# Attention with normalised queries and keys, then a two-layer MLP: a written-out schedule instead of a planner, with moved multiplies, sums and unused matmuls

## The chip, the cores and the metric

One core of a Trainium2 chip runs the whole program. The metric is the device time of one execution in microseconds (us), given as the median of several executions. The engines are named as the profile names them: PE is TensorE (matmuls; PEld is its weight load), DVE is VectorE, ACT is ScalarE, POOL is GpSimd, SP is the queue that issues most DMAs.

## The reference

```python
# q, k, v: (8, 12, 448, 64) float32; w_in: (768, 2048); w_out: (2048, 768)
def rmsnorm(x, g):
    rms = np.sqrt(np.mean(x * x, axis=-1, keepdims=True) + 1e-06)
    return x / rms * g
q_n, k_n = rmsnorm(q, g_q), rmsnorm(k, g_k)
scores = np.matmul(q_n, k_n.transpose(0, 1, 3, 2)) / np.sqrt(64)
scores = scores - np.max(scores, axis=-1, keepdims=True)
attn = np.exp(scores)
attn = attn / (np.sum(attn, axis=-1, keepdims=True) + 1e-09)
o = np.matmul(attn, v)                          # per batch and head
x = o.transpose(0, 2, 1, 3).reshape(3584, 768)  # heads side by side
h = x @ w_in
out = np.maximum(0.01 * h, h) @ w_out
```

## The kernel before

**Units.** A unit `u` is four heads of one batch; there are 24 (`NU`), three to a batch (`NQ`). The 448 keys of a head are cut into 7 tiles of 64. Per unit, q and k are loaded, squared (`prep_sq` on ACT or `prep_sqp` on POOL), summed (`prep_ssq`, DVE), turned into a factor (`prep_rinv`, ACT), multiplied (`prep_norm`, DVE), and transposed into `qkT` by PE (`prep_tr`) or by a DMA that SP issues (`prep_trd`). This is done one to three units ahead.

**Steps.** In the main loop a unit has four steps `d`, which hold the score tiles (0), (1, 2), (3, 4) and (5, 6). A step issues `qk` (PE, line 199: four matmuls of 64x64 for a tile, side by side in the array) and `ex` (ACT, line 218: exp of a tile of 128x896). The scores lie in one of two PSUM slots, so tile t can be written when the exp of tile t-2 has been read, and tile 1 of a unit needs the exp of tile 0. At step 0 stands the shift of the softmax: `shift_max` takes the maximum of tile 0 (DVE, line 236) and makes a diagonal of it (line 238), PE multiplies that (`shift_mm`, line 248, or 254 in the early units), DVE takes the second maximum (line 249 or 255), and line 257 gives the bias `eb` that every exp of the unit waits for. Between the two, PE runs the products with v of the unit before (`pv`, line 367) and the sums over exp (`zcol`, line 307). `pv_out` (ACT, line 322) copies the product out behind the second maximum, in front of the first exp. The reciprocal of the sums goes through ACT and a DMA (`zcol_inv`), and `xmul_pool`, `xmul_sb` or `xmul` writes the finished `xt` of the unit (line 347 on POOL or DVE, line 376).

**Items.** PE time between the steps is filled by the MLP of the batches before, cut into items in a queue: `moe1` (6 matmuls of 128x448, line 389, then a Prelu on ACT that writes `gt`), `moe2` (half of the sum for half an output tile, 8 matmuls of 128x384, line 430), and the items i0 to i6 of `seven` (8 matmuls of 128x384 each, line 471), which make two output tiles at once from seven products in place of eight. `seven` needs sums of blocks of `gt`, `s1` to `s4` (DVE, lines 452 to 461), and its results are merged by DVE adds (line 478). In the last two batches `moe1` is replaced in part by `late1` (line 591), a scheme of seven products too, with Prelu at line 601. What an item leaves for DVE, ACT and SP goes into a list `pend`, and `flush` runs it at the start of the next item or at the end of the step.

**Who decides the order.** The order is that of the program text on each engine. How many items a step takes is worked out by `fill`: each item has a cost (1.13 for `moe1`, 0.575 for `late1`, 1.31 for the others), each step a weight (`WD`), and the queue is spread over the steps left until the next batch is pushed. `fill` also holds the step's `jobs` (preparation of later units, multiplies): after each item one job is issued, and what is left follows at the end, behind `flush`. `warm` issues matmuls of which nothing is used. After unit 23 the rest of the queue and the last batch run as a tail; there `hold` makes the PSUM banks a hand-kept list that `drop` gives back to.

Of the kernel before, what the change touches and what calls it, by code (L numbers as in the profile page):

```python
# [18 lines left out]
def kernel(  # L19
# [13 lines left out]
    B, H, S, D = q.shape  # L33
# [4 lines left out]
    NU = B * NQ  # L38
# [373 lines left out]
    pend = []  # L412
    L, R, LR = slice(0, HC), slice(HC, DM), slice(0, DM)

    def flush():
        while pend:
            pend.pop(0)()

    def out_tile():
        return opool.tile([P, DM], FP32, tag="ost", name="ost")  # L420

    def moe2(pair, t, half, part):
        flush()
        if half == 0 and part == 0:
            ost[0] = out_tile()
        if part == 0:
            ost[1] = aux([P, 512], FP32, "op2")
        op2 = ost[1]
        for ft in range(8 * part, 8 * part + 8):
            nc.tensor.matmul(op2[:, 0:HC], gt[:, ft, ds(col(t), P)], wout16[:, ft, ds(HC * half, HC)],  # L430
                             start=(ft == 0), stop=(ft == FT - 1))
# [16 lines left out]
    def gblock(t, j):  # L448
        return gt[:, HF * j:HF * j + HF, ds(col(t), P)]
# [11 lines left out]
        nc.vector.tensor_tensor(sa[:, 3, x], gblock(tt[0], 1)[:, x], sa[:, 1, x], op=ALU.subtract)  # L461

    def later(fn, *args):
        pend.append(lambda: fn(*args))

    def seven(pair, tt, nxt=None, last=False):
        g = {}

        def mm(bank, a, b, first):
            for f in range(HF):  # L470
                nc.tensor.matmul(bank[:, 0:HC], a[:, f], b[:, f], start=(first and f == 0), stop=(f == HF - 1), skip_group_check=not first)  # L471

        def bank(name):
            g[name] = aux([P, 512], FP32, name)
            return g[name]

        def add(dst, src, name):
            nc.vector.tensor_tensor(dst, g[name][:, 0:HC], src, op=ALU.add)

        def put(i, c):  # L480
            store(pair, tt[i], g["o"][i], c, last)

        def i0():
            flush()
            g["o"] = (out_tile(), out_tile())
            mm(bank("ma"), gblock(tt[0], 0), wblock(0, 0), True)
            later(lambda: nc.vector.tensor_copy(g["o"][1][:, L], g["ma"][:, 0:HC]))

        def i1():
            flush()  # L490
            mm(bank("mb"), sa[:, 1], tw[:, 1], True)
            later(lambda: add(g["o"][1][:, L], g["o"][1][:, L], "mb"))
            later(lambda: drop(g["mb"]))

        def i2():
            flush()
            mm(g["ma"], gblock(tt[0], 1), wblock(1, 0), False)
            later(lambda: nc.scalar.copy(g["o"][0][:, L], g["ma"][:, 0:HC]))
            later(lambda: drop(g["ma"]))
            if last:  # L500
                later(put, 0, L)

        def i3():
            flush()
            mm(bank("mc"), sa[:, 0], tw[:, 0], True)
            later(lambda: add(g["o"][1][:, R], g["o"][1][:, L], "mc"))
            if nxt:
                later(s1, nxt)

        def i4():  # L510
            flush()
            mm(bank("md"), sa[:, 2], tw[:, 2], True)
            later(lambda: add(g["o"][1][:, R], g["o"][1][:, R], "md"))
            if last:
                later(put, 1, R)

        def i5():
            flush()
            mm(g["mc"], sa[:, 3], wblock(1, 1), False)
# [59 lines left out]
    def late1(b, tail, after):  # L579
# [45 lines left out]
        def item(n, s):  # L625
            flush()
            if not g:
                start()
            if n == 1:
                mm(get(1, s), 1, s, x_b(b, 0, 0), True)  # L630
                later(lambda: copy(tmp["u"][:, s % 2], g[1, s][:, 0:S]))
            elif n == 2:
                mm(get(2, s), 2, s, x_b(b, 1, 0), True)
                later(lambda: vadd(tmp["u"][:, s % 2], g[2, s], tmp["u"][:, s % 2]))
                later(lambda: drop(g[2, s]))
                later(lambda: out_(s, 0, 0, tmp["u"][:, s % 2]))
            elif n == 7:
                mm(get(7, s), 7, s, xs[3], True)
                later(lambda: nc.vector.tensor_copy(tmp["v"][:, s % 2], g[7, s][:, 0:S]))
            elif n == 6:  # L640
                mm(g[1, s], 6, s, xs[2], False)
                later(lambda: vadd(g[7, s][:, 0:S], g[1, s], tmp["v"][:, s % 2]))
            elif n == 5:
                mm(g[1, s], 5, s, xs[1], False)
                later(lambda: vadd(tmp["v"][:, s % 2], g[1, s], tmp["v"][:, s % 2]))
                later(lambda: out_(s, 1, 1, tmp["v"][:, s % 2]))
            elif n == 4:
                mm(g[7, s], 4, s, xs[4], False)
                later(lambda: out_(s, 1, 0, g[7, s][:, 0:S]))
                later(lambda: drop(g[7, s]))  # L650
            else:
                mm(g[1, s], 3, s, x_b(b, 1, 1), False)
                later(lambda: out_(s, 0, 1, g[1, s][:, 0:S]))
                later(lambda: drop(g[1, s]))
            for fn in after.get((n, s), ()):
                pend.append(fn)

        return item

# [14 lines left out]
    def push(b):  # L674
# [24 lines left out]
                    items.append((0.575, lambda w=w: item(*w)))  # L699
        if odd:  # L700
            tt, tn = (3, 4), (5, 6)
            items += [(1.31, fn) for fn in seven(pair, tt, tn)]
            for n, x, fs in ((len(items) - 7, 1, (s3, s4)),) if late else ((8, 0, (s1, s2)), (10, 0, (s3, s4)), (FT - 1, 1, (s1, s2)), (FT, 1, (s3, s4))):
                c, fn = items[n]
                items[n] = (c, also(fn, *[lambda f=f, x=x: later(f, tt, half[x]) for f in fs]))
            items += [(1.31, fn) for fn in seven(pair, tn, None, b == B - 1)]
        else:
            tiles = (2,) if fast else (0, 1, 2)
            std = [lambda t=t, h=h, p=p: moe2(pair, t, h, p) for t in tiles for h in range(2) for p in range(2)]
# [6 lines left out]
            items += [(1.31, fn) for fn in std]  # L716
        queue.extend(items)

    WD = (3.6, 2.9, 2.8, 2.8)
    STEPS = ((0,), (1, 2), (3, 4), (5, 6))  # L720
    debt = [0.0]

    def narrow(u):
        return 4 <= u < NU - 1
# [1 line left out]
    def fed(u, d):  # L726
        return u % NQ == 0 and d == 3

    def fill(u, d, jobs):
        total = sum(c for c, _ in queue)  # L730
        left = WD[d] + 3.0
        uu, dd = u, d
        while True:
            dd += 1
            if dd == 4:
                uu, dd = uu + 1, 0
            if uu == NU or (fed(uu, dd) and (u > 3 or uu > 3)):
                break
            left += WD[dd]
        debt[0] += total * WD[d] / left  # L740
        while queue and debt[0] >= queue[0][0] * 0.5:
            c, fn = queue.pop(0)
            fn()
            debt[0] -= c
            if jobs:
                jobs.pop(0)()
        flush()
        for job in jobs:
            job()

# [20 lines left out]
    with tc.manual_schedule():  # L771
# [150 lines left out]
        load_v(5)  # L922
        qk(2, (2,))
        ex(2)
        warm(6, st[2]["pb"])
        qk(2, (3,))
        ex(2)
        trn(3, 0, vcopy)
        trn(3, 1, vcopy)
        xmul(1)  # L930
        prep_ssq(4)
# [30 lines left out]
        for u in range(3, NU):  # L962
            for d in range(4):
                if d > 0 or u > 3:
                    qk(u, STEPS[d])
                    if d == 0:
                        shift_max(u)
                        if u == 6:
                            xmul_sb(u - 2)
                        if narrow(u - 1):  # L970
# [48 lines left out]
                if u + 2 < NU:  # L1019
# [72 lines left out]
```

## Time and profile before

| | |
|---|---|
| median of 4 runs | 417.25 us (416.98 to 417.43) |
| the profiled execution, its own time | 416.57 us |
| its span, from first to last instruction | 414.7 us |
| PE busy | 399.1 us, 96%, 3817 matmuls |
| DVE busy | 307.3 us, 74% |
| ACT busy | 300.7 us, 73% |
| POOL busy | 68.5 us, 17% |
| granted TensorE clock | 1.00 |

The profile is of one execution, and its times count from the start of the span. A row of the timeline gives start, duration, engine, line and operation, the tiles written and read, how many instructions were merged, and in brackets how long the engine had been idle and what released it. Matmuls are pipelined and the end of each is modelled, so the idle time in brackets is shorter than the hole in the stream: the hole is read from start to start.

### The profile page before, as it was taken

Reading aid. Unit: us, or ns where it says so; the run is one execution under the profiler, and the core shown is the slowest. Engines: PE = TensorE matmul, PEld = TensorE weight load, DVE = VectorE, ACT = ScalarE, POOL = GpSimd, SP = SyncE. Lnnn points to the kernel's source line nnn. Section 1 sums busy time; section 2 is a strip of 40 time slices with the busy share of each in tenths; the row PEclk is TensorE's granted clock in tenths of the full one; section 3 lists DMA queues with packets and bytes.
Section 4 is the critical chain, followed back from the end, with each engine's and each line's share of the span. In section 5 each row is a group of like instructions: output and inputs, shape, how many; then the busy total and the mean of one; then the engine's idle time right before and its main releaser. Section 6 shows DMA issues by size and latency. Waiting matters only on the chain.

```text
span 414.7 us, 9343 instructions
## 1 busy us (share of the span) xinstructions
PE 399.1 (96%) x3817; PEld 218.8 (53%) x3817; DVE 307.3 (74%) x492; ACT 300.7 (73%) x470; POOL 68.5 (17%) x70
## 2 busy tenths in 40 slices
PE   8688999999999999999999999999999999999995
PEld 7444444554445544555455544455445557558863
DVE  5888898998888757866668757767669788557762
ACT  5898887677987699767887689867986657653600
POOL 1868432200020200010020100020001202000000
PEclk9999999999999999999999999999999999999999
DMA  6999999989566995677664995678552470033023
GB/s 206 279 237 246 240 250 146 230 176 205 138 154 92 225 236 101 150 181 174 158 157 69 222 200 132 172 143 190 157 102 47 120 162 6 10 74 77 2 56 98
DMA packets 71950, 62.41 MB, mean 150 GB/s; under 512 B 36324, under 2 KB 67044, under 8 KB 71908
## 3 DMA queue, kind: packets, MB, share of 16 engines
q1 hardware_dynamic: 61312, 49.62, 47.6%
q0 software_dynamic: 10272, 11.80, 18.2%
q8 instruction: 30, 0.49, 0.5%
q10 hardware_dynamic: 324, 0.39, 0.3%
q14 instruction: 12, 0.10, 0.1%
HBM read 45.61 MB, written 11.01 MB: 137 GB/s over the span
## 4 chain that ended last, share of the span: by engine, by line
PE 82%; DVE 10%; ACT 5%; issue 1%; DMA 1%; SPq 0%; DVEq 0%
PE hps L389 27%; PE sT L199 8%; PE sT L367 5%; PE ma L471 5%; PE md L471 5%; PE mc L471 5%; PE op L430 5%; PE bank L591 4%; PE bank L471 4%; ACT et L218 3%; PE mb L471 3%; DVE n L171 3%; PE zc L307 2%; PE sT L471 2%; PE bank L430 1%
## 5 line engine op out<-in xcount | busy, mean ns | idle before, releaser
L218 ACT ACTIVATE et<-sT,eb 128x896 f16<-128x896 f32 x166 | 159.3, 1008 | 26.7 <-PE sT L199 17.4
L389 PE MATMUL hps<-xt,win 128*128 128x448 f16 x600 | 121.0, 353 | 0.3 <-DVE xt L376 0.2
L389 PEld LDWEIGHTS <-win 128*128 128x128 f16 x612 | 56.8, 98 | 58.4 <-issue 10.0
L383 ACT ACTIVATE gt<-hps 128x448 f16<-128x448 f32 x100 | 53.9, 554 | 7.4 <-PE hps L389 6.4
L199 PE MATMUL sT<-qkT 64*64 64x448 f16 x664 | 52.5, 363 | 4.1 <-ACT et L218 2.8
L159 DVE TENSOR_REDUCE ssq<-sq 128x14 f32<-128x896 f32 (+2 forms) x49 | 50.1, 1057 | 0.4 <-ACT sq L148 0.4
L471 PEld LDWEIGHTS <-sa 128*128 128x128 f16 x352 | 32.8, 98 | 26.3 <-issue 6.1
L128 POOL DMA_DIRECT2D vt<-in_v_dram x24 | 17.9, 746 | 172.0 <-PE sT L367 165.3
L471 PEld LDWEIGHTS <-gt 128*128 128x128 f16 x264 | 25.2, 98 | 19.0 <-issue 2.4
L199 PEld LDWEIGHTS <-qkT 64*64 64x64 f16 x672 | 15.3, 104 | 37.3 <-issue 32.6
L322 ACT COPY x<-sT 128x896 f32<-128x896 f32 x16 | 14.5, 906 | 25.7 <-DVE sT L249 25.7
L347 POOL TENSOR_TENSOR xt<-x,rz 128x896 f16<-128x896 f32 x9 | 18.9, 2099 | 79.9 <-DMA rz<-zs 71.5
L171 DVE TENSOR_TENSOR n<-rq,rinv 128x896 f16<-128x896 f32 (+2 forms) x25 | 26.7, 1073 | 5.0 <-ACT rinv L165 5.0
L292 DVE TENSOR_TENSOR ea<-ea,et 128x896 f16<-128x896 f16 x27 | 16.9, 625 | 16.5 <-ACT et L218 15.6
L367 PE MATMUL sT<-et,vt 64*64 64x448 f16 x532 | 28.5, 349 | 0.3
L430 PE MATMUL op<-wout,gt 128*128 128x384 f16 x160 | 28.4, 326 | 0.0
L236 DVE TENSOR_REDUCE sT<-sT 128x1 f32<-128x896 f32 x22 | 24.1, 1093 | 3.5 <-PE sT L199 3.5
L367 PEld LDWEIGHTS <-vt 64*64 64x64 f16 x672 | 20.5, 107 | 11.3 <-issue 1.4
L171 DVE TENSOR_TENSOR n<-rk,rinv 128x896 f16<-128x896 f32 (+2 forms) x26 | 26.1, 1010 | 0.0
L430 PEld LDWEIGHTS <-gt 128*128 128x128 f16 x192 | 17.6, 98 | 14.4 <-issue 3.1
L471 PE MATMUL ma<-wout,gt 128*128 128x384 f16 x128 | 23.5, 326 | 0.0
L292 DVE TENSOR_TENSOR ea<-et 128x896 f16<-128x896 f16 x14 | 9.4, 672 | 11.8 <-ACT et L218 11.7
(144 smaller groups left out, 548.5 us busy)
## 6 DMA issues: line engine op xcount, KB each, us to landing
rq<-in_q_dram SPq DMA_DIRECT2D x24, 448.0 KB, 4.3
rk<-in_k_dram SPq DMA_DIRECT2D x24, 448.0 KB, 5.7
out_dram<-ost SPq DMA_DIRECT2D x52, 192.0 KB, 3.1
rz<-zs SPq DMA_DIRECT2D x76, 112.0 KB, 2.3
vt<-in_v_dram POOLq DMA_DIRECT2D x24, 224.0 KB, 5.0
win<-in_moe_w_in_dram POOLq DMA_DIRECT2D x8, 384.0 KB, 15.9
wout<-in_moe_w_out_dram POOLq DMA_DIRECT2D x2, 1536.0 KB, 28.9
out_dram<-ost SPq DMA_DIRECT2D x4, 96.0 KB, 2.1
```

The source lines that it names most:

```text
L159: nc.vector.tensor_reduce(buf(u, "ssq")[:, ti, :, c[0]:c[1]], buf(u, f"sq{ti}")[:, :, c[0]:c[1]], axis=AXL.X, op=ALU.add)
L171: nc.vector.tensor_tensor(buf(u, "n16")[:, ti, c[0]:c[1]].rearrange("p s a d -> p a s d"), src[:, :, c[0]:c[1]], buf(u, "rinv")[:, ti, :, ...
L199: nc.tensor.matmul(banks[a][64 * r:64 * r + 64, 0:S].rearrange("p (t x) -> p t x", t=NS), kT(u, r, a, t), qT(u, r, a), start=True, stop=True)
L218: nc.scalar.activation(s["et"][:, t], sT[:, :, 0:S], AF.Exp, bias=s["eb"], scale=1.0)
L236: nc.vector.tensor_reduce(s["spare"][:, 511:512], sT[:, :, 0:S], axis=AXL.XY, op=ALU.max)
L292: nc.vector.tensor_tensor(s["ea"], s["et"][:, 0] if t == 1 else s["ea"], s["et"][:, t], op=ALU.add)
L347: eng.tensor_tensor(xts[b][:, g], s["x32"], s["rz"], op=ALU.mult)
L367: nc.tensor.matmul(s["pv"][r][64 * a:64 * a + 64, 0:S], vts[u % NV][64 * r:64 * r + 64, a, t], s["et"][64 * r:64 * r + 64, t, a], start=(t ...
L383: nc.scalar.activation(dst, src, AF.Prelu, bias=0.0, scale=1.0, alpha=0.01)
L389: nc.tensor.matmul(hps[:, 0:S], win16[:, kt // 2, kt % 2, ts(ft, P)], xt[:, kt // 2, kt % 2], start=(kt == 0), stop=(kt == KT - 1))
L430: nc.tensor.matmul(op2[:, 0:HC], gt[:, ft, ds(col(t), P)], wout16[:, ft, ds(HC * half, HC)], start=(ft == 0), stop=(ft == FT - 1))
L471: nc.tensor.matmul(bank[:, 0:HC], a[:, f], b[:, f], start=(first and f == 0), stop=(f == HF - 1), skip_group_check=not first)
```

## The change

The planner is replaced by a table `PLAN` of items per step. Against the counts that the planner gave, it differs in these places: in unit 3 one `moe1` item moves from step 1 to step 2 (2, 1 becomes 1, 2), in unit 4 one moves from step 0 and one from step 1, so that steps 0 to 2 hold 1, 2, 2 in place of 2, 2, 1; and one item each moves forward from step 0 of units 12, 16 and 18 to step 3 of units 11, 15 and 17 (1, 3 becomes 2, 2).

`flush(keep=True)` at the end of step 3 keeps `s1` to `s4` back, and a new `flush()` issues them behind `shift_max` of the next unit, so they stand between the first maximum and the second. This concerns `s3` and `s4` at units 8, 14 and 20 (half of the blocks) and at units 12 and 18 (all of them). When item i4 falls into step 2, no job is taken between it and the merges. The x multiply of unit 5 (`xmul_sb`) moves in front of two `prep_norm`. In the opening part, while unit 2's scores run, there are 6 more unused matmuls in one place and 8 in another. In the late batches `moe2` takes its 16 blocks in another order, and the first item of the last `seven` is mixed with the second. In the tail, half of the last `xmul` moves behind item i4.

```diff
-    def flush():
-        while pend:
-            pend.pop(0)()
+    def flush(keep=False):
+        kept = [p for p in pend if keep and p[0] in (s1, s2, s3, s4)]
+        now = [p for p in pend if p not in kept]
+        pend[:] = kept
+        for fn, args in now:
+            fn(*args)
...
-    def moe2(pair, t, half, part):
+    def moe2(pair, t, half, part, late=False):
...
-        for ft in range(8 * part, 8 * part + 8):
+        fts = (0, 1, 2, 3, 4, 5, 8, 9, 10, 12, 13, 11, 14, 15, 6, 7) if late else range(FT)
+        for i in range(8 * part, 8 * part + 8):
+            ft = fts[i]
             nc.tensor.matmul(op2[:, 0:HC], gt[:, ft, ds(col(t), P)], wout16[:, ft, ds(HC * half, HC)],
-                             start=(ft == 0), stop=(ft == FT - 1))
+                             start=(i == 0), stop=(i == FT - 1))
...
         def i0():
...
-            mm(bank("ma"), gblock(tt[0], 0), wblock(0, 0), True)
+            ma = bank("ma")
+            if mixed:
+                mm(ma, gblock(tt[0], 0), wblock(0, 0), True, range(6))
+                mm(bank("mb"), sa[:, 1], tw[:, 1], True, range(4))
+            mm(ma, gblock(tt[0], 0), wblock(0, 0), True, range(6 if mixed else 0, HF))
...
         def i1():
             flush()
-            mm(bank("mb"), sa[:, 1], tw[:, 1], True)
+            mm(g["mb"] if mixed else bank("mb"), sa[:, 1], tw[:, 1], True, range(4 if mixed else 0, HF))
...
+        i4.merges = True
...
-            items += [(1.31, fn) for fn in seven(pair, tt, tn)]
+            items += [(1.31, fn) for fn in seven(pair, tt, tn, mixed=late)]
...
-    WD = (3.6, 2.9, 2.8, 2.8)
+    PLAN = ("2122", "1222", "2112", "2122", "3232", "3322", "2322",
+            "2322", "3232", "2222", "3323", "3232", "2322", "2322",
+            "3232", "2222", "3323", "3232", "2322", "4356", "5232")
...
     def fill(u, d, jobs):
...
-        debt[0] += total * WD[d] / left
-        while queue and debt[0] >= queue[0][0] * 0.5:
-            c, fn = queue.pop(0)
+        for n in range(int(PLAN[u - 3][d])):
+            fn = queue.pop(0)[1]
             fn()
-            debt[0] -= c
-            if jobs:
+            if jobs and not (d == 2 and hasattr(fn, "merges")):
                 jobs.pop(0)()
-        flush()
+        flush(keep=d == 3 and u < NU - 1)
...
-        warm(6, st[2]["pb"])
+        warm(12, st[2]["pb"])
         qk(2, (3,))
         ex(2)
         trn(3, 0, vcopy)
+        warm(8, st[2]["pb"])
         trn(3, 1, vcopy)
...
                         shift_max(u)
+                        flush()
...
                         job(prep_rinv, u + 2)
+                        if u == 6:
+                            job(xmul_sb, u - 1)
                         for ti in range(2):
                             job(prep_norm, u + 2, ALL, (ti,))
...
-                if d == 2 and u == 6:
-                    job(xmul_sb, u - 1)
...
-        xmul(NU - 1)
-        for i, ns in enumerate(((3, 1), (2, 4))):
+        xmul(NU - 1, (0,))
+        for i, more in enumerate((((xmul, NU - 1, (1,)), (x_sum, B - 1, 3), (x_sum, B - 1, 1)), ((x_sum, B - 1, 2), (x_sum, B - 1, 4)))):
             c, fn = queue[i]
-            queue[i] = (c, also(fn, *[lambda n=n: later(x_sum, B - 1, n) for n in ns]))
+            queue[i] = (c, also(fn, *[lambda m=m: later(*m) for m in more]))
```

More of the change, by code (lines that the diff above doesn't have):

```diff
@@ L463, in later, with seven, mm @@
     def later(fn, *args):
-        pend.append(lambda: fn(*args))
-    def seven(pair, tt, nxt=None, last=False):
+        pend.append((fn, args))
+    def seven(pair, tt, nxt=None, last=False, mixed=False):
         g = {}
-        def mm(bank, a, b, first):
-            for f in range(HF):
+        def mm(bank, a, b, first, fs=range(HF)):
+            for f in fs:
                 nc.tensor.matmul(bank[:, 0:HC], a[:, f], b[:, f], start=(first and f == 0), stop=(f == HF - 1), skip_group_check=not first)
@@ L655, in item @@
             for fn in after.get((n, s), ()):
-                pend.append(fn)
+                later(fn)
         return item
@@ L708, in push @@
             tiles = (2,) if fast else (0, 1, 2)
-            std = [lambda t=t, h=h, p=p: moe2(pair, t, h, p) for t in tiles for h in range(2) for p in range(2)]
+            std = [lambda t=t, h=h, p=p: moe2(pair, t, h, p, late) for t in tiles for h in range(2) for p in range(2)]
             if fast:
@@ L717, in push @@
         queue.extend(items)
-    WD = (3.6, 2.9, 2.8, 2.8)
+    PLAN = ("2122", "1222", "2112", "2122", "3232", "3322", "2322",
+            "2322", "3232", "2222", "3323", "3232", "2322", "2322",
+            "3232", "2222", "3323", "3232", "2322", "4356", "5232")
     STEPS = ((0,), (1, 2), (3, 4), (5, 6))
-    debt = [0.0]
     def narrow(u):
@@ L729, in fill @@
     def fill(u, d, jobs):
[L730 to L739, printed above, removed]
-        debt[0] += total * WD[d] / left
-        while queue and debt[0] >= queue[0][0] * 0.5:
-            c, fn = queue.pop(0)
-            fn()
-            debt[0] -= c
-            if jobs:
+        for n in range(int(PLAN[u - 3][d])):
+            fn = queue.pop(0)[1]
+            fn()
+            if jobs and not (d == 2 and hasattr(fn, "merges")):
                 jobs.pop(0)()
-        flush()
+        flush(keep=d == 3 and u < NU - 1)
         for job in jobs:
```

## The prediction

> **What bounds the kernel now.** I read the page first, then the waits of PE, then the timeline around each place that the diff touches.
>
> ```profile
> span 414.7 us, 9343 instructions
> PE 399.1 (96%) x3817; PEld 218.8 (53%) x3817; DVE 307.3 (74%) x492; ACT 300.7 (73%) x470; POOL 68.5 (17%) x70
> ...
> PEclk9999999999999999999999999999999999999999
> ```
>
> PE is busy all the way at full clock, so a reordering can win no more than the holes in PE's stream. I measure a hole from start to start: a set of four 64x64 matmuls follows the last after 0.19 us, a 128x448 after 0.19, a 128x384 after 0.163. After the opening (to 45 us) and before the drain (from 410.5 us) few holes are left.
>
> ```profile
> PE sT L199 <- ACT et L218: 2.8, 7, 0.5
> ...
> PE bank L430 <- ACT gt L601: 0.5, 1, 0.5
> ...
> PE bank L471 <- ACT gt L601: 0.2, 1, 0.2
> PE hps L389 <- DVE xt L376: 0.2, 1, 0.2
> ```
>
> The waits of PE: mostly a score tile that waits for an exp. The timeline shows where, first units 3 and 4 (51.84 - 51.09 - 0.19 = 0.56 hole; 65.16 to 65.91 is the same in unit 4), with the DVE work behind it:
>
> ```profile
> 51.09 0.38 PE L199 MATMUL sT<-qkT 64*64 64x448 f16 x4
> ...
> 51.84 0.38 PE L199 MATMUL sT<-qkT 64*64 64x448 f16 x4 [0.37 <-ACT et L218]
> ```
> ```profile
> 54.34 1.08 DVE L171 TENSOR_TENSOR n<-rk,rinv 128x896 f16<-128x896 f32 x1
> ...
> 55.34 1.09 DVE L236 TENSOR_REDUCE sT<-sT 128x1 f32<-128x896 f32 x1
> ...
> 56.47 0.29 DVE L238 TENSOR_TENSOR dg<-ident,sT 128x128 f16<-128x128 f16 x1
> ...
> 56.81 0.23 PE L254 MATMUL pb<-dg,onesp 128*128 128x128 f16 x1
> ```
>
> Unit 12, where one item moves out of step 0 and the sums go between the two maxima:
>
> ```profile
> 171.95 0.38 PE L199 MATMUL sT<-qkT 64*64 64x448 f16 x4
> ...
> 172.44 1.52 PE L367 MATMUL sT<-et,vt 64*64 64x448 f16 x28
> ...
> 174.27 0.71 POOL L128 DMA_DIRECT2D vt<-in_v_dram  x1 [14.25 <-PE sT L367]
> 174.60 0.22 PE L248 MATMUL sT<-dg,onesp 128*128 128x64 f16 x2
> ...
> 174.86 0.30 DVE L249 TENSOR_REDUCE sT<-sT 128x1 f32<-128x128 f32 x1 [0.31 <-PE sT L248]
> 175.19 0.91 ACT L322 COPY x<-sT 128x896 f32<-128x896 f32 x1 [1.13 <-DVE sT L249]
> ...
> 175.27 0.68 DVE L458 TENSOR_TENSOR sa<-gt 128x1024 f16<-128x1024 f16 x1
> ...
> 175.99 1.01 ACT L218 ACTIVATE et<-sT,eb 128x896 f16<-128x896 f32 x1
> ```
>
> The holes there: 0.28 in front of 172.44 (pv's slot waits for an exp) and 0.21 in front of 174.60 (line 248 waits for the diagonal, whose maximum stood behind `s2`). And ACT's copy, then the first exp, hang on the second maximum.
>
> **The change part by part.** PE does the same matmuls, plus 14 unused ones. The holes at the touched places: 0.56 in unit 3; 0.56 in unit 4; 0.29 at 93.9 (the first `moe1` of batch 1 waits for xt of unit 5: six matmuls take 93.16 to 94.67 where 1.22 would do); 0.49 in unit 12; 0.28 in unit 16 (236.15 to 236.64); 0.49 in unit 18 (as unit 12); 0.63 at 358.12 (six matmuls from 356.51 would end at 357.49); 0.37 at 393.09 (391.74 + 0.98 = 392.72); 0.23 at 374.34 (372.81 + 1.30 = 374.11). Sum 3.91 us, the most there is. Now each:
>
> *Unit 3.* With one item less in step 1, tile 4 is asked for 1.13 earlier, at 48.40; the exp of tile 2 ends at 48.13, so no hole. With two items in step 2, tile 6 comes at 51.26 and the exp of tile 4 ends near 50.65. The hole is gone, but DVE is the next: it is busy without a gap from 46.8 to 55.4 (sums of squares, `add_e`, two norms), so the first maximum of unit 4 stays at 55.34, the diagonal at 56.47, and line 254 at 56.81, where PE now waits 0.6. Gain 0 (at most 0.56).
>
> *Unit 4.* Unit 3's end stays, so step 0 starts as before; step 0 has one item less and the hole at 65.91 is covered by the second item of step 2 (tile 6 at 65.32, exp of tile 4 ends near 64.8). DVE follows this time: its norms end near 67.9, PE's tile for the maximum of unit 5 comes at 68.0 in place of 68.6. Gain 0.56.
>
> *x multiply of unit 5.* DVE is free for it at 91.06; the last of its four rz DMAs is issued near 88.2 and lands 2.3 us later, at 90.5. It ends at 92.1, 1.8 us before the fifth matmul. The norms behind it and the transposing DMA on SP go 1.0 us later, and behind that SP only has stores; the maximum of unit 7 (PE-bound, now at 94.9) finds DVE free at 94.6. Gain 0.29.
>
> *Units 12 and 18.* Let Q be the start of step 0's tile. Two items before Q let the exp finish: 0.28 won. `s2` is out before Q, so the maximum is PE-bound; as in unit 8 (110.43 to 112.07) the diagonal starts at Q + 1.64 and PE, which gets to line 248 at Q + 2.14 (112.57 there), doesn't wait: 0.21 won. But `s3` and `s4` now follow the diagonal: from Q + 1.84 (0.20 behind it, as 82.84 to 83.04), 0.60 each by the rows 175.27 and 175.87, so the second maximum starts at Q + 3.05, not Q + 2.41. The first exp gives its slot back 2.1 us after that (1.13 to 1.19 to its start, 0.90 on), at Q + 5.15. PE with two items comes at Q + 4.90 (unit 9, also two of 1.30, took 126.73 to 131.73, with 0.10 more of `zcol`). New wait 0.25: net 0.24 each, 0.48 together. ACT's work on the reciprocal and the rz DMAs go about 1.5 us later; the stores that now stand ahead of them on SP are issued by then, and the POOL multiply has until 191.7. Beside it a norm takes 1.68 in place of 1.08, for which unit 13 has 0.4 of slack: 0 to 0.2.
>
> *Units 8, 14, 20.* Half sums of 0.34 each: the second maximum at Q + 2.52, the slot back at Q + 4.62, PE with three items at Q + 5.71 (110.43 to 116.14). Nothing.
>
> *Unit 16.* Becomes what unit 10 is (two items, no sums), which has no hole: gain 0.28.
>
> *Late `moe2`.* Its first eight blocks are all written by 356; those of line 601 come last, at 359.4, and are ready at 358.06. Behind it, tile 1 of unit 23 needs an exp that ended at 356.05. Gain 0.63.
>
> *Mixed i0.* Four matmuls of i1 fill the 0.37. But i1's other four need `s2`, which still ends at 393.94 (Prelu 393.03, `s1`, `s2` of 0.42 each). They started at 394.07 before, and now at 394.0. Gain 0.07.
>
> *Tail multiply.* With half of `xmul` behind it, the merge that i6 waits for ends 0.5 earlier, so i6 starts at 374.11. The sums of x end as before to 0.1. Gain 0.23.
>
> *Costed at nothing.* The 14 unused matmuls, 0.057 each: 0.34 into the 0.55 hole at 33.49 (wait for zslot), 0.46 into the 0.60 at 34.82 (wait for a norm); without that cover 0.8. They bring nothing, the granted clock there is 1.00 already. i4's merge ahead of the norms (units 9, 12, 15, 18, 21): norm k and its transposing DMA end some 0.45 later, and the readers are the `qkT` scaling and sums of squares of step 1, whose results wait a step; up to 0.4 if that cover fails.
>
> Sum: 0.56 + 0.29 + 0.48 + 0.28 + 0.63 + 0.07 + 0.23 = 2.54. The profiled execution's own time is 416.57 (span 414.7 and 1.87 around it), so it would be 414.03; the median, 417.25, stands 0.68 above it and becomes 414.7.
>
> **A rule against this change.** DVE sums whose operands lie in SBUF can be held by POOL. In the trace the same line 458 of 128x512 takes 0.42 alone but 1.85 beside POOL's multiply (120.97, POOL at 120.37). The sums' new place, Q + 1.84 to Q + 3.05, is where POOL issues the load of v (Q + 2.04, 0.71 long). The Trainium skill, "SBUF — State Buffer", section "SBUF: two separate sides", says that DVE and GpSimd share a port pair as an exclusive lock held for a whole instruction, and that descriptor writing for a POOL-issued DMA needs it. By the rule `s4` could be held for the issue: some 0.8 more at units 12 and 18, a wait of 1.05 there, and a total of 2.54 - 1.6 = 0.9. The nearest row speaks for no hold: the multiply of two SBUF operands at 83.04 took 1.08 beside such an issue at 82.75, as alone; but it is float32, not a fast f16 sum. I take no hold, and keep 0.9 for the range.
>
> **The rivals.**
> - *More comes.* If DVE's chain in unit 3 shortens, or the second maximum isn't late: 2.54 + 0.56 = 3.1, at most 3.9: 414.2 to 413.35. Against it: the gapless DVE row up to 55.34. 12%.
> - *The lock holds, or a norm or merge comes late.* 0.9 to 1.7 gained: 416.35 to 415.55. 21%.
> - *It does not do what it says.* ACT or a DMA, not PE, sets the pace, and every hole closed opens at the next exp as in unit 3: within 0.8 of 417.25. Against it: holes of ACT (0.59 before several Prelus) follow PE. 6%.
> - *Slower: the held sums.* One mechanism: each pair of moved sums is held h, and the second maximum, ACT's copy and the first exp with it. Units 12 and 18 then wait 0.25 + h each (0.49 before), units 8, 14 and 20 wait h - 1.06. Against the other gains of 2.06 that is even at h = 1.14 and 0.83 slower from h = 1.31. With the hold of the row at 120.97 (1.43) it is 418.7. A v issue lasts 0.71 to 0.76, so h should stay below that. 3%.
>
> **How the numbers follow.** The forecast, with its own range of 414.2 to 415.4, has 58%. A measurement here can tell about 0.2%, 0.83 us, from no change: under 416.42 is faster. Faster: 58 + 12 + 19 of the second rival = 0.89; same 0.08; slower 0.03. The range leaves out part of the first rival and the last two: 413.4 to 416.4.
>
> **What would show it.** Right: no hole at the steps 3 of units 3 and 4, but PE waiting about 0.6 for the diagonal (line 254) in unit 4; in units 12 and 18 a new wait of about 0.3 of tile 1 for the first exp; no wait at the late `moe2`; about 0.3 for `s2` in i1. Wrong: `s3` or `s4` far longer than 0.68 or 0.42, the second maximum over 1 us after line 248, or new PE waits in units 8, 14, 20 or 13.

## The result, and the profile after

The changed kernel takes 416.55 us (median of 44 runs, 415.34 to 418.12), the kernel before 417.20 on the same chips (63 runs). The ratio is 0.9983, with a 95% interval of 0.9978 to 0.9989: 0.7 us gained (0.5 to 0.9), where 2.54 were forecast. It lies just outside the forecast range (413.4 to 416.4).

From the page of the changed kernel, the lines that answer to those of before:

```profile
span 415.2 us, 9374 instructions
PE 399.9 (96%) x3831; PEld 220.0 (53%) x3831; DVE 309.0 (74%) x492; ACT 300.0 (72%) x470; POOL 69.1 (17%) x70
...
PEclk9899999999999999999999999999999999999999
```

The span is longer than before (414.7), which the medians contradict. The reason is in slice 2 of the clock row, and the table of windows shows it (window, its length, PE, PEld, DVE, ACT and POOL busy with the number of instructions in brackets, then the granted clock, the DMA share and GB/s):

```profile
12.00:16.00 4.00, 2.67 (x34) 1.71 (x34) 3.66 (x7) 3.69 (x8) 3.27 (x4) 1.00 1.07 343
16.00:20.00 4.00, 3.16 (x34) 1.99 (x34) 2.89 (x6) 3.28 (x4) 4.00 (x6) 0.77 1.18 224
20.00:24.00 4.00, 4.00 (x63) 2.49 (x65) 3.37 (x8) 3.37 (x6) 2.58 (x5) 0.80 1.07 242
24.00:30.00 6.00, 4.67 (x72) 2.78 (x61) 5.44 (x8) 5.93 (x9) 3.31 (x3) 1.00 1.12 230
```

This execution had a reduced clock between 16 and 24 us, and the third matmul of line 254 came 1.25 us later than in the profile of before (0.60 of it was there by the first one, at 12 us). In the thirteen profiles besides that of before, the same matmul stands 0.07 to 2.09 us behind that of before; 0.07 to 0.87 where the clock stays at 1.00, 0.57 to 2.09 where it dips. So the opening differs between executions, and the work after it must be compared by itself. I do that from the matmul of line 254 in unit 4 to the last instruction: 357.9 us before, 357.1 after, a gain of 0.78 that agrees with the medians.

Where PE waits now (its waits: total, times, longest):

```profile
PE sT L199 <- ACT et L218: 2.1, 5, 0.5
PE sT L248 <- DVE dg L238: 2.0, 2, 1.4
PE pb L254 <- DVE dg L238: 1.6, 3, 0.6
...
PE sT L476 <- DVE sa L460: 0.2, 1, 0.2
```

Two of these were forecast: unit 4's wait for the diagonal (0.6, the longest of the three in the third line) and i1's wait for `s2` (the fourth line). The second line was not: 2.0 us in two places in front of line 248, in units 13 and 19. Start to start these holes are 0.68 and 1.43 us. The prediction had named a new wait in unit 13 as a sign of its being wrong. This is the end of unit 18 and the start of unit 19 on DVE, POOL and PE, in the timeline of the changed kernel:

```profile
280.36 0.56 DVE L483 TENSOR_TENSOR ost<-md,ost 128x384 f32<-128x384 f32 x1 [0.74 <-PE md L476]
280.83 1.08 DVE L171 TENSOR_TENSOR n<-rq,rinv 128x896 f16<-128x896 f32 x1
280.94 2.93 POOL L347 TENSOR_TENSOR xt<-x,rz 128x896 f16<-128x896 f32 x1 [9.41 <-DMA rz<-zs]
281.83 2.98 DVE L171 TENSOR_TENSOR n<-rk,rinv 128x896 f16<-128x896 f32 x1
...
285.86 1.09 DVE L236 TENSOR_REDUCE sT<-sT 128x1 f32<-128x896 f32 x1
...
286.98 0.29 DVE L238 TENSOR_TENSOR dg<-ident,sT 128x128 f16<-128x128 f16 x1
287.32 0.22 PE L248 MATMUL sT<-dg,onesp 128*128 128x64 f16 x2 [1.37 <-DVE dg L238]
```

And the same place in the kernel before:

```profile
277.17 2.08 POOL L347 TENSOR_TENSOR xt<-x,rz 128x896 f16<-128x896 f32 x1 [7.09 <-DMA rz<-zs]
279.84 1.09 DVE L171 TENSOR_TENSOR n<-rq,rinv 128x896 f16<-128x896 f32 x1 [0.31 <-ACT rinv L165]
281.32 1.08 DVE L171 TENSOR_TENSOR n<-rk,rinv 128x896 f16<-128x896 f32 x1
283.95 1.09 DVE L236 TENSOR_REDUCE sT<-sT 128x1 f32<-128x896 f32 x1
```

Before, POOL's x multiply was over (279.25) when the first norm began. Now it starts at 280.94, because `rz` landed later. The second norm takes 2.98 us instead of 1.08, and two merges, the maximum, the diagonal and line 248 follow it. Unit 13 is the same on a smaller scale: POOL at 184.96, the first norm 2.23 long.

By place, the prediction's sum and the profile:

| place | forecast gain | measured |
|---|---|---|
| unit 3, unit 4 | 0, 0.56 | 0, 0.56 |
| x multiply of unit 5 | 0.29 | 0.28 |
| units 12 and 18, each | 0.24 | 0.35 |
| unit 16 | 0.28 | 0.28 |
| late `moe2` | 0.63 | 0.63 |
| mixed i0 | 0.07 | 0.05 |
| tail multiply | 0.23 | 0.10 |
| unit 21 (hole of 0.19 before line 248 gone) | none | 0.19 |
| unit 13 | 0 to -0.2 | -0.68 |
| unit 19 | not named | -1.43 |
| sum | 2.54 | 2.80 - 2.11 = 0.69 |

### The profile page after: what moved, and what is told of

Its sections match the earlier page's. It is cut to its first block, busy times and chain, and to the rows that moved or that the text cites. A ratio compares the mean times of both kernels' runs of the same rounds, so it can differ in the third digit from the quotient of the medians.

```text
span 415.2 us, 9374 instructions
## 1 busy us (share of the span) xinstructions
PE 399.9 (96%) x3831; PEld 220.0 (53%) x3831; DVE 309.0 (74%) x492; ACT 300.0 (72%) x470; POOL 69.1 (17%) x70
## 4 chain that ended last, share of the span: by engine, by line
PE 84%; DVE 9%; ACT 4%; issue 2%; DMA 1%; SPq 0%; DVEq 0%
PE hps L389 27%; PE sT L199 9%; PE op L435 6%; PE sT L367 5%; PE ma L476 5%; PE bank L602 5%; PE bank L476 5%; PE mc L476 5%; PE md L476 4%; DVE n L171 4%; PE mb L476 3%; PE zc L307 2%; ACT et L218 2%; PE sT L476 1%; PE bank L435 1%
## 5 line engine op out<-in xcount | busy, mean ns | idle before, releaser
L171 DVE TENSOR_TENSOR n<-rk,rinv 128x896 f16<-128x896 f32 (+2 forms) x26 | 28.0, 1084 | 0.0
L148 ACT ACTIVATE sq<-rq 128x896 f32<-128x896 f32 (+2 forms) x18 | 16.3, 913 | 1.3 <-DMA rq<-in_q_dram 1.3
```

What stands on the lines that cost most here:

```text
L171: nc.vector.tensor_tensor(buf(u, "n16")[:, ti, c[0]:c[1]].rearrange("p s a d -> p a s d"), src[:, :, c[0]:c[1]], buf(u, "rinv")[:, ti, :, ...
```

## The experiments

The theory to test, S: the held sums `s3`, `s4` make the second maximum of units 12 and 18 late, with it ACT's copy and the reciprocal, so `rz` is issued later (in these units also behind two output stores on SP that stood behind it before). POOL's multiply then falls beside the norms and blocks them. Rivals: M, the merge moved ahead of the norms is enough to delay the maximum; O, the opening takes the gain back through the additional unused matmuls. D, F and C came later and are explained in their place. The flight of `rz` is the time from the start of its first DMA packet to the end of its last. In the expectations, times of an instruction fetch and of a flight count from an origin 0.25 us later than the timeline's.

**rz ahead of the stores.** `zcol_inv` is issued at once in two units, so `rz` stands ahead of the two stores on SP.

```diff
-                        if u < NU - 1:
+                        if u in (12, 18):
+                            zcol_inv(u - 1)
+                        elif u < NU - 1:
                             job(zcol_inv, u - 1)
```

> The changed kernel, with one thing moved: in units 12 and 18 the reciprocal and its four rz DMAs are issued ahead of step 0's first item, so that on SP they stand ahead of the two stores again, as before the change. Theory S (the stores ahead of rz on SP, with the later second maximum, make POOL's multiply late, and it then lies beside the two norms of DVE, which hold the maximum of units 13 and 19): POOL's multiply starts 1.9 us after the last rz issue, near 184 in unit 12 and 279.2 in unit 18 (184.96 and 280.94 now); the norms beside it take at most 0.6 more than 1.08 (now 1.15 and 1.90 more), PE's waits in front of line 248 in units 13 and 19 fall from 0.68 and 1.43 to 0.1 to 0.4 each: 1.3 to 1.9 us less than the changed kernel, 414.7 to 415.3. Theory M (the merge moved ahead of the norms alone makes the maximum late): no change, 416.5, both waits as now. Theory O (the opening takes back the gain, by the 14 more unused matmuls): no change of the total either, 416.5.

Measured: 415.33 us, ratio 0.9959 (0.9947 to 0.9970). A part of it came: unit 13 doesn't wait any more, unit 19 waits 1.32. Timeline of this kernel, unit 12 and then unit 18:

```profile
183.15 2.08 POOL L347 TENSOR_TENSOR xt<-x,rz 128x896 f16<-128x896 f32 x1 [7.57 <-DMA rz<-zs]
184.88 1.31 DVE L171 TENSOR_TENSOR n<-rq,rinv 128x896 f16<-128x896 f32 x1
...
279.11 2.08 POOL L347 TENSOR_TENSOR xt<-x,rz 128x896 f16<-128x896 f32 x1 [9.14 <-DMA rz<-zs]
279.28 2.87 DVE L171 TENSOR_TENSOR n<-rq,rinv 128x896 f16<-128x896 f32 x1
```

Read the ends: POOL ends at 185.23 and the norm at 186.19; POOL at 281.19, the norm at 282.15. Each norm ends 0.96 us after POOL, whenever it began. My expected excess of "at most 0.6" was wrong: a norm that meets the multiply waits for whatever is left of it.

What the order saved is not what I thought. The rows of SP alone in unit 12, in the changed kernel and here:

```profile
178.00 1.17 SPq L409 DMA_DIRECT2D out_dram<-ost  x2
179.59 3.46 SPq L337 DMA_DIRECT2D rz<-zs  x4
```
```profile
178.71 2.57 SPq L337 DMA_DIRECT2D rz<-zs  x4
181.33 1.25 SPq L409 DMA_DIRECT2D out_dram<-ost  x2
```

Both issues of `rz` begin 3.74 us after line 248, when ACT has the reciprocal. But in the changed kernel the first packet of `rz` moves 2.17 us after that, behind packets of the stores (179.18 to 182.06) and an instruction fetch among them (179.17 to 180.73); here after 1.20. In unit 18 these are 1.24 and 1.21, so there was nothing to save there. The multiply comes 0.94 us earlier against line 248 in unit 12, and 0.26 in unit 18. There the issue of `rz` was over at 275.61, but the multiply began 3.5 us later, not 1.9; so something else delays the landing.

**Sums behind the second maximum.**

```diff
                         shift_max(u)
-                        flush()
...
                             shift_mm(u)
+                            flush()
```

> The changed kernel with the held sums s3 and s4 not behind the first, but behind the second maximum and its bias. Theory S: the second maximum of units 12 and 18 comes 1.2 us earlier, 0.31 after line 248; tile 1's waits for the first exp (0.14 each) go; the stores still stand ahead of rz on SP, so that rz starts only 0.4 earlier and POOL's multiply by as much: 0.3 to 0.9 us less than the changed kernel, 415.7 to 416.3, with 0.4 to 1.2 left of the wait in unit 19. A rival, that the late second maximum alone is the cause: both waits go, 414.2. Theory M: only the 0.28 of the two tile waits, 416.3.

Measured: 415.89 us, ratio 0.9981 (0.9970 to 0.9992), not to be told from the changed kernel. Both waits of tile 1 are gone and the second maximum follows line 248 directly again, but the stores hold `rz` up instead; units 13 and 19 wait 0.86 and 1.09. So the late maximum alone is not the cause, and unit 13's wait did not shrink as S had it.

**The merge behind the first norm again.**

```diff
-            if jobs and not (d == 2 and hasattr(fn, "merges")):
+            if jobs:
```

> The changed kernel with i4's merge behind the first norm again, as before the change (units 9, 12, 15, 18, 21). Theory S: the first norm of units 12 and 18 starts 0.4 to 0.9 us earlier and the maximum behind it 0.35 to 0.47, since the idle time of DVE in front of that norm is used: 0.5 to 0.9 us less than the changed kernel, 415.6 to 416.0; the norms still take 1 to 1.9 us more beside POOL. Theory M: both waits in front of line 248 go, 2.1 us less, 414.4. If the move of the merge was of use somewhere (units 9, 15, 21): 0.2 to 0.4 more in these, seen as new waits there.

Measured: 415.63 us, ratio 0.9968 (0.9957 to 0.9979). Waits of 0.54 and 0.54: smaller, not gone, so M alone is out, and the moved merge has a share in the waits. (The median itself can't be told from that of the changed kernel's second run, below.) Unit 12 here shows the other direction of the conflict:

```profile
183.68 1.09 DVE L171 TENSOR_TENSOR n<-rq,rinv 128x896 f16<-128x896 f32 x1 [0.32 <-ACT rinv L165]
183.86 2.86 POOL L347 TENSOR_TENSOR xt<-x,rz 128x896 f16<-128x896 f32 x1 [8.59 <-ACT rinv L165]
...
185.16 2.52 DVE L171 TENSOR_TENSOR n<-rk,rinv 128x896 f16<-128x896 f32 x1
```

The norm began first and took its 1.09; POOL's multiply was the one that was stretched, to 2.86 from 2.08, and the next norm then waited for it.

**Without the additional unused matmuls.**

```diff
-        warm(12, st[2]["pb"])
+        warm(6, st[2]["pb"])
...
-        warm(8, st[2]["pb"])
```

> The changed kernel without its 14 additional unused matmuls. Theory S: the opening of the changed kernel's profile (1.25 us later than before by 20 us, all of it ahead of these matmuls) is chance of that execution, and the 14 matmuls lie in waits: the time stays at 416.5 within 0.2, waits of 0.55 and 0.60 near 34 to 36 us instead of 0.22 each. Theory O: 1.2 us less, 415.3. If they keep the clock up behind them: more, and a granted clock under 1.00 after 35 us.

Measured: 414.94 us, ratio 0.9956 (0.9941 to 0.9971). S said no change here, and missed by 1.6 us. But O isn't right either: at the place of these matmuls nothing was won (unit 4's line 254 stands 0.09 behind that of before in this profile, 0.12 in the run with the merge moved back, which has the matmuls). What differs is unit 19, which doesn't wait: POOL's multiply started there at 278.19, counted from unit 18's line 248 that is 1.6 us earlier than in the changed kernel. The DMA queues show why. This is the changed kernel while `rz` of unit 18 is in flight, 275.9 to 280.1 (queue, packets, MB, share of 16 engines):

```profile
q1 hardware_dynamic: 816, 0.86, 80.6%
q8 instruction: 1, 0.02, 2.0%
q14 instruction: 1, 0.01, 0.5%
```

A packet of 16 KB of instructions falls into it. There are 30 of these in a run, 0.9 to 1.8 us long, and from one to the next PE runs 253 of its 7662 matmuls and weight loads on average, so I take them for PE's instruction fetches (7662 / 30 = 255 instructions each). `rz` goes in 512 packets of 896 bytes, and POOL waits for the last. With a fetch inside, the flight of `rz` in unit 18 took 3.3 to 4.4 us (eight profiles); without, 2.65 to 2.77 (six). Theory F: 28 PE instructions more, matmuls and weight loads, move the fetches earlier against the work, and in unit 18 into that flight. Theory D: the matmuls cost time directly. C: they keep the clock up.

**The unused matmuls alone, on the kernel before** (the two `warm` lines of the change).

> The kernel before with the 14 additional unused matmuls of the change and nothing else. Theory D (direct price): the run without them was 1.6 us faster than the changed kernel, so they cost about 1 us wherever they stand: 418.2. Theory F (they cost nothing where they run, but move PE's instruction fetches of 16 KB, one per 256 PE instructions, some 1.5 us earlier against PE's work; in unit 18 of the changed kernel one such fetch, 277.75 to 279.12, then lies in the flight of rz, 275.66 to 279.88, and POOL's multiply is late): here rz of unit 18 flies from 273.8 to 276.4 and the multiply stands behind it with slack, so the time stays at 417.1 within 0.3. Theory C (they keep the clock): 416.6 or less.

Measured: 417.02 us, ratio 0.9994 (0.9982 to 1.0006). No price, and no gain clear of noise: D is out. C's 416.6 lies at the edge of the interval, but the granted clock after 24 us is 1.00 with these matmuls and without, and without them the changed kernel was faster, not slower. The fetch of unit 18 came after `rz`. One hole did go in its profile, the 0.19 before line 248 in unit 21, which the kernel before has.

**Both edits: rz ahead of the stores, sums behind the second maximum.**

> The changed kernel with both edits: s3 and s4 behind the second maximum, and in units 12 and 18 rz on SP ahead of the two stores. Theory S: rz is issued at about 177.5 and 273.3 in place of 179.59 and 274.66, POOL's multiply starts near 182.3 and 277.7 (up to 279.3 where an instruction fetch falls into the flight of rz), that is at least partly ahead of the first norm; no wait of tile 1, no wait in unit 13, 0 to 1.0 in unit 19: 1.7 to 2.5 less than the changed kernel, 414.1 to 414.9. If the collision with the norm isn't what makes the waits: 416.2.

Measured: 414.79 us, ratio 0.9945 (0.9928 to 0.9963). Unit 13: no wait, both norms 1.08. Unit 19: 1.05, with a fetch in the flight of `rz` (4.35 us long). As S and F have it.

**And without the unused matmuls.**

> As the run before, and without the 14 additional unused matmuls. Theory F: the fetch falls behind the flight of rz in unit 18, the wait in unit 19 is gone in any case: 0 to 1.0 less than the run before, 414.0 to 414.3. Theory D: 1 us less than the run before whatever the fetch does. Either is the sum of all gains of the prediction, 2.54 to 2.8 under the kernel before.

Measured: 414.25 us, ratio 0.9927 (0.9910 to 0.9944). The best of all: 3.0 us faster than before. Its timeline in unit 18, and the queues during the flight of `rz` (274.0 to 276.7), with no q8 in it:

```profile
277.25 2.08 POOL L347 TENSOR_TENSOR xt<-x,rz 128x896 f16<-128x896 f32 x1 [6.96 <-ACT et L218]
279.45 1.08 DVE L171 TENSOR_TENSOR n<-rq,rinv 128x896 f16<-128x896 f32 x1
280.45 1.08 DVE L171 TENSOR_TENSOR n<-rk,rinv 128x896 f16<-128x896 f32 x1
282.65 1.09 DVE L236 TENSOR_REDUCE sT<-sT 128x1 f32<-128x896 f32 x1
```
```profile
q1 hardware_dynamic: 584, 0.49, 80.7%
q14 instruction: 1, 0.01, 0.7%
```

POOL ends at 279.33, 0.12 ahead of the norm. In unit 12 the first norm is still held (1.44 long), within the slack. PE waits nowhere in units 12, 13, 18 and 19. What the prediction's sum promised is there once the multiply is out of the norms' way.

**The changed kernel again.**

> The changed kernel again, for a second profile and on the same chip as these. If the opening of its first profile (1.25 us late by 20 us) was chance, it is another here, and the same kernel's waits in units 13 and 19 vary only with when rz lands: each wait is the excess of the norms over 2 x 1.08, less 0.47. Time 416.5 within 0.3. If the opening belongs to the kernel: 1.2 us late again.

Measured: 416.32 us, ratio 0.9972 (0.9963 to 0.9982). Opening 0.60 late this time, waits of 0.49 and 1.13 for norms that are 0.95 and 1.60 too long: the excess less 0.47. The same difference holds in every profile with a wait whose merge stands ahead of the norms. The same code thus gave 416.55 in one set of runs and 416.32, just inside the forecast range, in another; their intervals overlap.

**The unused matmuls moved into the opening**, and **left out once more**, on one chip.

```diff
-        warm(10, st[0]["pb"])
+        warm(15, st[0]["pb"])
...
-        warm(12, wb)
+        warm(17, wb)
...
-        warm(8, wb)
+        warm(12, wb)
...
-        warm(12, st[2]["pb"])
+        warm(6, st[2]["pb"])
...
-        warm(8, st[2]["pb"])
```

> The changed kernel with its 14 additional unused matmuls taken from 33 to 36 us to the opening: 5, 5 and 4 more in three runs of unused matmuls at 10 to 14 us, ahead of waits of 0.76, 0.69 and 0.66 there. Theory F (only their number counts, since it sets where PE's instruction fetches fall): as the changed kernel, 416.2 to 416.6, with the fetch of unit 18 in the flight of rz (over 3.7 us from its first to its last packet) and 0.9 to 1.5 of wait in unit 19. Theory D (they cost time where the change put them): as the run without them, 414.9.

> The changed kernel without the 14 unused matmuls once more, on the same chip as the run with them moved. Theory F: 414.9 to 415.3, the fetch of unit 18 behind or at the end of the flight of rz (2.7 us long), wait in unit 19 at most 0.5. If the first run of it was chance: 416.5.

Measured: 415.93 us, ratio 0.9970 (0.9959 to 0.9981), with them moved; 415.24, ratio 0.9951 (0.9938 to 0.9964), without. The first is a little under its expected 416.2 to 416.6, but its profile is that of the changed kernel: fetch in the flight of `rz`, flight of 3.73 us, waits of 0.54 and 1.09. Without them the flight is 2.76 with the fetch behind it, and unit 19 doesn't wait. So it is their number and not their place: F. The two intervals just overlap; what decides is that the profiles differ in the fetch and the wait, here and in the first run without them.

**The sums not held.**

```diff
-        flush(keep=d == 3 and u < NU - 1)
+        flush()
```

> The changed kernel with s3 and s4 not held: they run at the end of step 3, ahead of the first maximum. Theory S: in units 12 and 18 the first maximum starts 0.66 later (DVE reaches it at 269.95 in place of 269.29 in unit 18), PE waits 0.6 to 0.7 in front of line 248 there, but the second maximum still comes 0.5 earlier and the waits of tile 1 (0.14 each) go; rz stays behind the stores, so the waits in units 13 and 19 are those of the run with the sums behind the second maximum (0.86 and 1.09) or less: 416.3 to 417.2, no better than the changed kernel. If holding the sums was itself what made units 13 and 19 wait: both waits go, 415.3.

Measured: 416.13 us, ratio 0.9972 (0.9958 to 0.9986). Line 248 waits 0.41 in units 12 and 18 (0.6 to 0.7 expected), 0.58 in unit 13, 1.39 in unit 19. In its profile that is worse than the changed kernel; the median says slightly better, and the two cannot be told apart. What stands is that issuing the sums earlier doesn't remove the waits: the stores still stand ahead of `rz`, and a fetch lies in its flight.

**The best, with the merge behind the norm again.**

> The run with rz ahead of the stores, the sums behind the second maximum and no additional unused matmuls (414.25), and i4's merge behind the first norm again. Theory S: the first norm of units 12 and 18 starts near 184.2 and 278.4 in place of 185.20 and 279.45 and meets POOL's multiply (183.6 and 277.3 to 279.3): it ends 0.95 after POOL does, 1.4 and 0.9 more than alone, but it began 0.8 to 1.0 earlier, so the maximum comes within 0.3 of where it was and there is 0 to 0.4 of wait: 414.0 to 414.7. If the merge's place matters by itself: 0.7 more or less.

Measured: 415.09 us, ratio 0.9955 (0.9943 to 0.9968), outside what S said (414.0 to 414.7). No wait in front of line 248, but a new one in unit 12, start to start 1.13:

```profile
183.89 2.07 POOL L347 TENSOR_TENSOR xt<-x,rz 128x896 f16<-128x896 f32 x1 [7.98 <-ACT uu L164]
184.17 2.74 DVE L171 TENSOR_TENSOR n<-rq,rinv 128x896 f16<-128x896 f32 x1 [0.32 <-ACT rinv L165]
...
186.83 0.55 DVE L483 TENSOR_TENSOR ost<-md,ost 128x384 f32<-128x384 f32 x1
...
187.43 1.46 PE L476 MATMUL md<-tw,gt 128*128 128x384 f16 x8 [0.96 <-DVE ost L483]
```

The merge stands behind a norm that waits for POOL, and i6 needs `md` to be read before it can add to it. That is what the moved merge is good for: it keeps PE out of the conflict.

All runs, with the gain of the one profile (from unit 4's line 254 to the end) beside the gain of the medians (1 less the ratio, times 417.2):

| kernel | unit 13, 19 wait | profile | medians (interval) |
|---|---|---|---|
| changed | 0.68, 1.43 | 0.78 | 0.71 (0.46 to 0.92) |
| changed again | 0.49, 1.13 | 1.27 | 1.17 (0.75 to 1.54) |
| unused moved | 0.54, 1.09 | 1.27 | 1.25 (0.79 to 1.71) |
| rz first | 0, 1.32 | 1.58 | 1.71 (1.25 to 2.21) |
| sums behind second | 0.86, 1.09 | 1.24 | 0.79 (0.33 to 1.25) |
| merge back | 0.54, 0.54 | 1.80 | 1.34 (0.88 to 1.79) |
| no more unused | 0.72, 0 | 1.81 | 1.84 (1.21 to 2.46) |
| the same again | 0.47, 0 | 2.39 | 2.04 (1.50 to 2.59) |
| sums not held | 0.58, 1.39 | 0.41 | 1.17 (0.58 to 1.75) |
| rz and sums | 0, 1.05 | 2.13 | 2.29 (1.54 to 3.00) |
| the same, no more unused | 0, 0 | 3.16 | 3.05 (2.34 to 3.75) |
| best, merge back | 0, 0 | 1.94 | 1.88 (1.33 to 2.38) |

Read by columns, the two waits have different causes. Unit 13's is gone in the four kernels with `rz` ahead of the stores, and is 0.47 to 0.86 in the eight others. Unit 19's is gone in the four kernels with no fetch in the flight of `rz` in unit 18, and is 0.54 to 1.43 in the eight others. The late second maximum, where S began, decides neither by itself: "rz first" keeps it and unit 13 doesn't wait, "sums behind second" lacks it and both wait. So S is right from the late landing of `rz` on, and what makes it late is the stores in unit 12 and a fetch in unit 18.

## Why the prediction was wrong

The gains were sized well: every term that was costed as a gain came within 0.13 us, and together, with 0.19 in unit 21 that was not foreseen, they are 2.80 where 2.54 was forecast. The 14 unused matmuls lay in their cover as said (holes of 0.55 and 0.60 became 0.22 each), and the sums beside the issue of v were not held (0.68 and 0.68 in unit 18 beside an issue of 0.71).

The step that failed is in *Units 12 and 18*: "the stores that now stand ahead of them on SP are issued by then, and the POOL multiply has until 191.7. Beside it a norm takes 1.68 in place of 1.08, for which unit 13 has 0.4 of slack: 0 to 0.2." Unit 13 was costed at 0 to 0.2 and unit 19 at nothing; they cost 0.68 and 1.43. The row of the kernel before from which the price was taken:

```profile
183.40 2.07 POOL L347 TENSOR_TENSOR xt<-x,rz 128x896 f16<-128x896 f32 x1 [8.42 <-ACT et L218]
...
184.75 1.68 DVE L171 TENSOR_TENSOR n<-rq,rinv 128x896 f16<-128x896 f32 x1 [0.31 <-ACT rinv L165]
```

Four things were wrong in this step.

- The price. 1.68 was taken as what a norm costs beside the multiply. It was only what was left of the multiply in that row: POOL ends at 185.47 and the norm at 186.43, 0.96 later. In the profiles here 23 norms met a multiply and lost to it, and each ended 0.95 us after it. A multiply that starts with the norm costs it about 1.9 (2.98 in place of 1.08 in unit 18). The right term was: POOL's end, plus 0.95, against when the norm would have ended.
- The stores. They were issued in time, as said (until 179.17, `rz` from 179.59), but their packets were not gone, and with `rz` ahead of them unit 13 doesn't wait.
- The lateness. Moving `rz` by 1.5 us was named, but only for the reader of `xt` ("until 191.7"). The multiply's other partner, the norm that excludes it, was not asked. Counted back from where the next unit's line 248 would stand without its wait, the multiply came 1.5 us later than before in unit 12, but 3.7 in unit 18. The 1.5 agrees with the forecast by luck: the issue of `rz` came 1.8 later, the stores' packets added 1.0, and a fetch that had stretched the flight by 1.2 before was gone from it.
- The fetch of instructions. It makes up 1.6 us of these 3.7 (flight of 4.22 us, 2.66 before), and in the eight profiles that show it the flight was 0.6 to 1.7 us longer. Where it would fall after the change could not be read off the profile of before. That it stretches a flight could: in unit 12 of the kernel before one lies in it (180.84 to 182.02), and the flight takes 3.87 us. With 1.2 us less the multiply would have ended near 184.3, ahead of the norm whose 1.68 became the price.

The prediction did weigh the rule, at the wrong pair. The Trainium skill, "SBUF — State Buffer", section "SBUF: two separate sides", says that a DVE operation with two SBUF inputs and a GpSimd operation that reads SBUF exclude each other, and that whichever starts first keeps the ports for its whole instruction. The runs agree in both directions: norms held until POOL's end, and POOL held by a norm that began first (2.86 and 2.93 against 2.08). I asked it of `s4` against the issue of v, where the trace shows no hold, and not of the norm against the multiply, where the very row that I took a price from was the evidence. By the rule, with `rz` 1.5 us later as the prediction had it, unit 12's multiply would have lasted to 187.0 (185.47 + 1.5) and the first norm to 187.9, where it would have ended at 186.3 alone (184.75 + 0.45 for the merge + 1.08): 1.6, less 0.4 of slack, is 1.2 lost. In unit 18 the multiply would have ended at 280.75 (277.17 + 1.5 + 2.08), and the norm, behind its merge, starts about then: nothing lost. The forecast would have been a gain of 1.3, or 415.9, still without the fetch.

The rival "the lock holds, or a norm or merge comes late" is the nearest to what happened, with a range (415.55 to 416.35) that ends 0.2 short. Its name holds two mechanisms: a hold of the moved sums, which did not come, and a late norm, which did, by the same lock.

The prediction's holes add up to 3.90, not 3.91, which changes nothing. Of the smaller misses: the tail multiply brought 0.10, since a wait of 0.13 for a merge follows at 377.71 (line 602). Tile 1's new wait is 0.14, not 0.25, and stays what was forecast in kind. Unit 21's hole of 0.19 went because the sum in unit 20 met a multiply with less of itself left (312.86, 1.30 long, against 311.34, 1.93 long, before), which was not looked for. That is luck of the fetch, not a gain of the new order: before, the flight of `rz` there had a fetch in it (3.41 us, 2.65 in the changed kernel). The kernel before with the unused matmuls alone has no such hole either, and the first run without them has one of 0.37. Without this 0.19 the gains of the new order are 2.61.

What stays open: why the opening differs between executions, and why the fetch moves by 0.7 to 3.1 us, not by one amount, when 14 matmuls are added.

## What to carry to other kernels

When a transfer or a wait is moved, ask of the engine that it feeds not only who reads its result, but which operation runs beside it at the new time. An operation that is held by another ended a fixed time after it here (0.95 us for a norm, 0.28 for a sum of f16 halves); so a stretched row in the profile gives no price, but a rule, read from the ends of both rows. A DMA that is issued in time can still stand behind the packets of the one issued before it. And where a kernel hides such small DMAs with under a microsecond of slack, a change of PE's instruction count ahead of it can use the slack up, as the 14 unused matmuls did at 10 to 14 us as well as at 33 to 36.

## What the runs showed of the hardware

- Norms on DVE (float32 by float32, f16 out, both in SBUF) and POOL's multiply exclude each other: the 23 norms that met one and lost ended 0.95 us after POOL; a norm that began first held POOL (2.86 and 2.93 against 2.08). A sum of f16 halves is held alike (312.86, 1.30 long, ends 0.28 after POOL). A reduction of one operand is not: line 159 took 2.07 for two beside the multiply at 277.17 in the kernel before, as elsewhere.
- An instruction fetch holds up data: there are 30 packets of 16 KB in a run, 0.9 to 1.8 us each. With one in the flight of the 448 KB of `rz`, that flight took 3.3 to 4.4 us in unit 18, in place of 2.7. Over all units and profiles, 54 flights with a fetch inside had a median of 3.3 us (2.4 to 4.4), and 212 without one of 2.66, twelve of these over 2.9.
- TensorE's granted clock can fall in the opening of an execution, and not in the next one of the same code: 0.77 and 0.80 from 16 to 24 us in the changed kernel's profile, 0.64 and 0.50 in the second profile without the unused matmuls (opening 2.09 us late), 1.00 in the first. What decides it is open.
